# Odd heads' rows moved inside SBUF instead of repacked through DRAM, in a windowed-attention and MLP kernel

## The chip, the cores and the metric

The kernel runs on one core of one Trainium2 chip. The metric is the device time of one execution in microseconds (us).

Engines: PE multiplies matrices (PEld is its weight load), ACT applies activation functions, DVE is the vector engine, POOL is GpSimd, and SP (SyncE) issues the DMAs here. Each follows its own list of instructions, and between them they wait on semaphores.

## The reference

Two layers, each run twice with the same weights: attention over the last 256 positions with 32 heads of 16 numbers, and an MLP with GELU.

```python
def _A_ref(x, wqkv, wo):                      # x: 1 x 2048 x 512
    H = 32; Dh = 16; W = 256
    q, k, v = split(x @ wqkv)
    scores = einsum(q, k) * Dh ** -0.5        # masked to 0 <= i - j < W
    o = softmax(scores) @ v
    return o.reshape(B, S, D) @ wo
def _B_ref(x, w1, b1, w2, b2):                # F = 1792
    return gelu(x @ w1 + b1) @ w2 + b2

x = x + _A_ref(_layernorm(x), ...)
x = x + _B_ref(_layernorm(x), ...)            # both lines run twice
```

## The kernel before

Two parts matter. The first is the end of attention for one group of 8 heads and 256 queries; there are 64 groups. PV (the exponentials times the values) writes each head to a block of 17 PSUM rows at partition 32r, r = 0 to 3: 16 outputs, and in row 16 the sum of the exponentials (the value matrix has a column of ones). Even heads lie in the left half of the free axis (a = 0), odd heads in the right (a = 1). The output projection wants 128 dense rows, 8 heads times 16. So the group is copied to SBUF (OD) and repacked, while the sums take their own way.

```python
evac(lambda B: OD[:, s, :, :], ..., ["OD%d" % s], kind="o")        # s = group % 3; ACT or DVE
dma(Dc[:, rs, :] <- OD[16:P:32, s]  ("r a (k n) -> r (a k) n"))     # the sums, 8 KB; assumed 2.2 us
dma(scr[rs].rearrange("j r n -> r j n") <- OD[:, s])                # 256 KB to DRAM; assumed 3.8 us
add("dve", reciprocal(Rc[:, rs, :], Dc[:, rs, :]), prio=pr - 800)
dma(scr_r[rs] <- Rc[:, rs, :])                                      # 8 KB to DRAM; assumed 2.0 us
dma(On[:, rs, :] <- scr[rs, 0:Dh]   ("j r (a q) -> (j r a) q"))     # 128 KB, dense; assumed 2.3 us
dma(Rn[:, rs, :] <- scr_r[rs][None, :, :].to_broadcast([Dh, HC, 2*P]))  # 128 KB; assumed 2.8 us
add("pool", OT[:, bs, c, :] = On[:, rs, :] * Rn[:, rs, :], alt=dve) # POOL or DVE, input of the projection
```

(Written down shortly: `dma(a <- b)` stands for a helper with the same two access patterns. Dc holds the sums and Rc their reciprocals, Rn the reciprocals spread over 128 rows, On the repacked outputs, scr and scr_r are scratch in DRAM, scr_o in the profile; OT is the normalised output. "Dc landed" means that the DMA into Dc is complete.)

The second part is how the order of instructions comes about. The program is a graph of nodes with an assumed duration each. While the kernel is built, an ordering pass plays the graph through with these durations, and always starts the most urgent node that is ready:

```python
class _Plan:
    LAT = {"pe": 230.0, "act": 110.0, "dve": 110.0, "pool": 150.0, "sp": 100.0}
    def add(self, eng, fn, dur, reads=(), writes=(), prio=0.0, ...): ...
    def run(self):
        ...                                    # pick by priority among ready nodes
        nd["start"] = t
        end = t + dur
        efree[e] = t + nd["geo"] if e == "sp" else end     # geo: time to issue a DMA
        order.append(pick)
        ...
```

The result is one fixed list per engine. At run time nothing is picked again: if an instruction's input is late, all behind it on its engine wait (the timeline of POOL below shows a case).

The softmax here doesn't subtract the row's maximum and nothing guards it: scores larger than these inputs give would overflow.

## Time and profile before

| | before |
|---|---|
| time, median of 3 runs | 682.63 us (680.83 to 683.09) |
| profiled execution | 678.0 us |
| mean granted PE clock | 0.899 |

From the profile's page of the kernel before: busy time with its share of the span and the number of instructions, then the chain of waits, by engine and by line.

```profile
PE 516.0 (76%) x4945; PEld 250.9 (37%) x5008; DVE 368.4 (54%) x766; ACT 471.5 (70%) x701; POOL 269.2 (40%) x456
...
DMA 41%; PE 27%; ACT 15%; DVE 7%; SPq 5%; issue 3%; POOL 2%; DVEq 0%; POOLq 0%
DMA scr_o<-OD 22%; PE ps L544 21%; ACT E L647 13%; DMA Rn<-scr_r 12%; DMA scr_r<-Rc 5%; PE ps L690 3%; PE ps L634 2%; SPq L706 2%; PE ps L528 2%; SPq L715 1%; DMA X<-in_A_x_dram 1%; ACT OD L500 1%; DVE X L553 1%; DVE OT L723 1%; SPq L718 1%
```

No engine is full, and the chain is mostly DMA, half of it the store of the repack. Where PE idles stands in the groups of instructions; after the second bar is the idle time just before the group and what ended most of it. L634 is the scores, L690 is PV, L544 with Wo_sb the output projection, L528 the transposes of the normalised rows.

```profile
L634 PE MATMUL ps<-QT,KT 32*128 32x384 bf16 (+2 forms) x1024 | 92.1, 346 | 42.8 <-ACT E L647 41.6
...
L690 PE MATMUL ps<-E,Va 128*17 128x128 bf16 (+1 forms) x1920 | 60.5, 273 | 37.1 <-POOL E L660 16.6 <-DVE KT L588 7.0 <-DVE E L652 5.7
...
L544 PE MATMUL ps<-Wo_sb,OT 128*128 128x512 bf16 x120 | 36.7, 442 | 33.2 <-DVE OT L723 12.2 <-POOL OT L720 8.9 <-DVE Rc L711 6.4
...
L528 PE MATMUL ps<-ident,xn 128*128 128x128 bf16 x256 | 28.1, 245 | 23.5 <-DVE xn L520 20.9 <-DVE QT L498 1.5 <-DVE Va L498 0.8
```

Some matmul records are missing here (120 of 128 for Wo), so the idle times are a little too long.

Who waited for whom (total us, times, longest), kernel before; first the engines, then the DMA queue's own waits:

```profile
DVE OT L723 <- DMA Rn<-scr_r: 99.0, 30, 7.3
POOL OT L720 <- DMA Rn<-scr_r: 91.6, 29, 15.4
ACT E L647 <- PE ps L634: 85.5, 42, 23.7
```

```profile
SPq L715 <- DMA scr_o<-OD: 186.7, 61, 5.3
```

DVE and POOL stand still 191 us in total in front of OT, with 59 waits. SyncE spends 187 us waiting for the store before it may issue On. One group in the timeline of the DMA issues of the kernel before (start, duration of the issue, what):

```profile
285.90 0.58 SPq L706 DMA_DIRECT2D Dc<-OD  x1
286.52 0.55 SPq L709 DMA_DIRECT2D scr_o<-OD  x1
288.60 0.49 SPq L713 DMA_DIRECT2D scr_r<-Rc  x1
292.39 0.32 SPq L715 DMA_DIRECT2D On<-scr_o  x1
292.76 0.58 SPq L718 DMA_DIRECT2D Rn<-scr_r  x1
```

SyncE has nothing to do between 289.1 and 292.4: it waits until the store of 286.52 has landed, 5.87 us later. What one blocked OT does is best seen in the timeline of POOL, kernel before (the bracket: idle time before, and what ended it):

```profile
324.87 1.23 POOL L660 TENSOR_SCALAR_AFFINE_SELECT E<-E 128x512 bf16<-128x512 bf16 x2
334.69 0.72 POOL L720 TENSOR_TENSOR OT<-On,Rn 128x256 bf16<-128x256 f32 x1 [8.59 <-DMA Rn<-scr_r]
335.37 0.64 POOL L660 TENSOR_SCALAR_AFFINE_SELECT E<-E 128x512 bf16<-128x512 bf16 x1
```

The mask at 335.37 stood behind OT. PV needed the mask, and PE idled 8.5 us before it.

### The profile page before, as it was taken

Reading aid. Unit: us, or ns where it says so; the run is one execution under the profiler, and the core shown is the slowest. Engines: PE = TensorE matmul, PEld = TensorE weight load, DVE = VectorE, ACT = ScalarE, POOL = GpSimd, SP = SyncE. Lnnn points to the kernel's source line nnn. Section 1 sums busy time; section 2 is a strip of 40 time slices with the busy share of each in tenths; the row PEclk is TensorE's granted clock in tenths of the full one; section 3 lists DMA queues with packets and bytes.
Section 4 is the critical chain, followed back from the end, with each engine's and each line's share of the span. In section 5 each row is a group of like instructions: output and inputs, shape, how many; then the busy total and the mean of one; then the engine's idle time right before and its main releaser. Section 6 shows DMA issues by size and latency. Waiting matters only on the chain.

```text
span 678.0 us, 12448 instructions
## 1 busy us (share of the span) xinstructions
PE 516.0 (76%) x4945; PEld 250.9 (37%) x5008; DVE 368.4 (54%) x766; ACT 471.5 (70%) x701; POOL 269.2 (40%) x456
## 2 busy tenths in 40 slices
PE   3854778779467996799487988689768996589857
PEld 2421344344233433444133433434324433233524
DVE  6963646537474566735384666645565455624221
ACT  0497486859857897668486797669868795758503
POOL 5584333626533266312472265523544154401010
PEclk9975698989879998799798998799989998689979
DMA  9512221212322023212222022211322023211310
GB/s 291 176 49 74 71 65 28 56 49 55 77 64 64 18 65 81 66 31 67 64 67 63 18 72 68 57 47 45 93 73 66 21 79 83 70 55 43 85 41 23
DMA packets 47132, 45.38 MB, mean 67 GB/s; under 512 B 14049, under 2 KB 38370, under 8 KB 47074
## 3 DMA queue, kind: packets, MB, share of 16 engines
q1 hardware_dynamic: 47074, 44.59, 24.5%
q8 instruction: 39, 0.64, 0.4%
q14 instruction: 19, 0.16, 0.1%
HBM read 24.65 MB, written 19.40 MB: 65 GB/s over the span
## 4 chain that ended last, share of the span: by engine, by line
DMA 41%; PE 27%; ACT 15%; DVE 7%; SPq 5%; issue 3%; POOL 2%; DVEq 0%; POOLq 0%
DMA scr_o<-OD 22%; PE ps L544 21%; ACT E L647 13%; DMA Rn<-scr_r 12%; DMA scr_r<-Rc 5%; PE ps L690 3%; PE ps L634 2%; SPq L706 2%; PE ps L528 2%; SPq L715 1%; DMA X<-in_A_x_dram 1%; ACT OD L500 1%; DVE X L553 1%; DVE OT L723 1%; SPq L718 1%
## 5 line engine op out<-in xcount | busy, mean ns | idle before, releaser
L647 ACT ACTIVATE E<-ps 128x768 bf16<-128x768 f32 (+2 forms) x512 | 353.3, 786 | 87.3 <-PE ps L634 85.5
L660 POOL TENSOR_SCALAR_AFFINE_SELECT E<-E 128x512 bf16<-128x512 bf16 x221 | 162.2, 739 | 155.9 <-ACT E L647 155.5
L775 ACT ACTIVATE gT<-ps,b1T 128x512 bf16<-128x512 f32 (+1 forms) x140 | 81.3, 604 | 80.0 <-PE ps L544 79.5
L652 DVE TENSOR_TENSOR E<-E,mask 128x512 bf16<-128x512 bf16 x210 | 99.4, 476 | 48.5 <-ACT E L647 46.8
L634 PE MATMUL ps<-QT,KT 32*128 32x384 bf16 (+2 forms) x1024 | 92.1, 346 | 42.8 <-ACT E L647 41.6
L544 PE MATMUL ps<-W_sb,gT 128*128 128x512 bf16 x412 | 113.3, 388 | 4.2 <-issue 4.0
L544 PE MATMUL ps<-xnTB,W_sb 128*128 128x512 bf16 (+1 forms) x557 | 107.8, 343 | 2.3 <-DVE Va L498 1.1
L690 PE MATMUL ps<-E,Va 128*17 128x128 bf16 (+1 forms) x1920 | 60.5, 273 | 37.1 <-POOL E L660 16.6
L544 PE MATMUL ps<-xnTA,Wqkv_sb 128*128 128x256 bf16 x512 | 77.7, 299 | 7.3 <-DVE xnTA L498 3.1
L544 PEld LDWEIGHTS ps<-xnTB,W_sb 128*128 128x128 bf16 x560 | 54.1, 99 | 47.0 <-issue 5.1
L634 PEld LDWEIGHTS ps<-QT,KT 32*128 32x128 bf16 x1024 | 26.0, 92 | 121.0 <-ACT E L647 108.7
L553 DVE TENSOR_TENSOR X<-X,ps 128x512 bf16<-128x512 bf16 x64 | 43.7, 682 | 49.8 <-PE ps L544 49.5
L723 DVE TENSOR_TENSOR OT<-On,Rn 128x256 bf16<-128x256 f32 x33 | 16.1, 487 | 99.0 <-DMA Rn<-scr_r 99.0
L690 PEld LDWEIGHTS ps<-E,Va 128*17 128x17 bf16 x1920 | 42.3, 98 | 60.6 <-issue 21.0
L544 PE MATMUL ps<-Wo_sb,OT 128*128 128x512 bf16 x120 | 36.7, 442 | 33.2 <-DVE OT L723 12.2
L720 POOL TENSOR_TENSOR OT<-On,Rn 128x256 bf16<-128x256 f32 x31 | 24.6, 792 | 91.6 <-DMA Rn<-scr_r 91.6
L514 POOL TENSOR_SCALAR veps<-statmv 128x1 f32<-128x1 f32 x64 | 15.0, 235 | 112.3 <-DVE statmv L512 112.2
L544 PEld LDWEIGHTS ps<-xnTA,Wqkv_sb 128*128 128x128 bf16 x512 | 49.0, 106 | 28.6 <-issue 6.0
L544 PEld LDWEIGHTS ps<-W_sb,gT 128*128 128x128 bf16 x448 | 37.3, 98 | 49.4 <-issue 21.1
L528 PE MATMUL ps<-ident,xn 128*128 128x128 bf16 x256 | 28.1, 245 | 23.5 <-DVE xn L520 20.9
L510 DVE BATCH_NORM_STATS2 stat<-X 128x6 f32<-128x512 bf16 x64 | 43.5, 683 | 2.5 <-DMA X<-in_A_x_dram 2.0
L588 DVE TENSOR_TENSOR KT<-ps,parmask 128x1024 bf16<-128x1024 f32 x32 | 38.1, 1209 | 6.8 <-PE ps L544 6.8
(36 smaller groups left out, 366.8 us busy)
## 6 DMA issues: line engine op xcount, KB each, us to landing
scr_o<-OD SPq DMA_DIRECT2D x64, 256.0 KB
On<-scr_o SPq DMA_DIRECT2D x64, 128.0 KB
Rn<-scr_r SPq DMA_DIRECT2D x64, 128.0 KB
W_sb<-in_B_w_dram SPq DMA_DIRECT2D x2, 1792.0 KB
out_dram<-X SPq DMA_DIRECT2D x16, 128.0 KB
Wqkv_sb<-in_A_wqkv_dram SPq DMA_DIRECT2D x3, 512.0 KB
X<-in_A_x_dram SPq DMA_DIRECT2D x1, 1024.0 KB
Dc<-OD SPq DMA_DIRECT2D x64, 8.0 KB
```

What stands on the lines that cost most here:

```text
L510: add("dve", lambda e, B: e.bn_stats(stat6[:, k, :], X[:, t, :]), 620, reads=["X%d" % t], writes=["st%d" % k], prio=prio)
L528: r = e.transpose(psb[:, B[g][0], c * P : (c + 1) * P], xn[:, s, c * P : (c + 1) * P], ident[:])
L544: r = e.matmul(ps[:, B[g][0], cols], lhsT, rhs, start=st, stop=sp)
L553: add("dve", lambda e, B: e.tensor_tensor(out=X[:, t, :], in0=X[:, t, :], in1=ps[:, B[g][0], :], op=ALU.add), d_psum(512), reads=["X%d" % ...
L588: add("dve", lambda e, B, g=g, i=i: e.tensor_tensor(out=KT[:, kb, :, 2 * i : 2 * i + 2, :].rearrange("p a c q -> p a (c q)"), in0=ps[:, B[ ...
L634: x = e.matmul(ps[:, bk[r], 0:N], KT[rows, kb, par, c, j * P : (j + 1) * P], QT[rows, c, q0 : q0 + N], start=True, stop=True)
L647: a = (add("act", lambda e, B, g=g, gi=gi: e.activation(E[:, es, 2 * gi : 2 * gi + 2, 0:N], ps[:, B[g][0] : B[g][0] + 2, 0:N], AF.Exp, sca ...
L652: add("dve", lambda e, B: e.tensor_tensor(out=E[:, es, :, 0:P], in0=E[:, es, :, 0:P], in1=mask01[:, None, 0, :].to_broadcast([P, RG, P]), ...
L660: add("pool", lambda e, B: e.affine_select(E[:, es, :, 2 * P : 3 * P], E[:, es, :, 2 * P : 3 * P], [[0, RG], [-1, P]], ALU.is_ge, 0.0, bas ...
L690: x = e.matmul(ps[32 * r : 32 * r + VW, B[g][0], par * 256 + q_lo * P : par * 256 + (q_hi + 1) * P], Va[:, (2 * b + k) % VR, h, :], E[:, e ...
L720: add("pool", lambda e, B: e.tensor_tensor(out=OT[:, bs, c, :], in0=On[:, rs, :], in1=Rn[:, rs, :], op=ALU.mult), 750, reads=["On%d" % rs, ...
L775: gelu_last[0] = add("act", lambda e, B, g=g, fc=fc: e.activation(gT[:, fc, 0:M], ps[:, B[g][0], 0:M], AF.Gelu_apprx_tanh, bias=b1T[:, fc ...
```

## The change

Intent: leave out the trip through DRAM. Even heads already lie at partitions 32r to 32r+15. If the odd heads' 16 rows are moved up 16 partitions, to 32r+16 to 32r+31 of the left half, the rows are dense in the natural order. Row 16 of the left half holds the even heads' sum, so a move must wait until Dc has been read. OD now lives until OT is made, hence 5 buffers instead of 3. Rn is read in the new order, Wo with one plain load. The DMAs of the sums and reciprocals became more urgent for the ordering (`prio=pr - 50`), and the moves come after them. The assumed durations of the new nodes were chosen anew, so the static order differs on every engine.

```diff
-        OD = sb("OD", [P, 3, 2, 2 * P], dt.float32)
-        On = sb("On", [P, DC, 2 * P], dt.float32)
+        OD = sb("OD", [P, NOD, 2, 2 * P], dt.float32)                 # NOD = 5
...
-                dma(lambda e, B: e.dma_start(scr[rs].rearrange("j r n -> r j n"), OD[:, s].rearrange("p a q -> p (a q)")),
-                    ["S%d" % rs], reads=["OD%d" % s], prio=pr, dur=3800.0)
...
                 dma(lambda e, B: e.dma_start(scr_r[rs].rearrange("h (k n) -> (h k) n", n=32), Rc[:, rs, :]),
-                    ["SR%d" % rs], reads=["Rc%d" % rs], prio=pr, dur=2000.0)
-                dma(lambda e, B: e.dma_start(
-                    On[:, rs, :], scr[rs, 0:Dh].rearrange("j r (a q) -> (j r a) q", a=2)),
-                    ["On%d" % rs], reads=["S%d" % rs], prio=pr + 2, dur=2300.0)
-                dma(lambda e, B: e.dma_start(Rn[:, rs, :], scr_r[rs][None, :, :].to_broadcast([Dh, HC, 2 * P])),
-                    ["Rn%d" % rs], reads=["SR%d" % rs], prio=pr, dur=2800.0)
+                    ["SR%d" % rs], reads=["Rc%d" % rs], prio=pr - 50, dur=2000.0, issue=490.0)
+                dma(lambda e, B: e.dma_start(Rn[:, rs, :], scr_r[rs][:, None, :].to_broadcast([HC, Dh, 2 * P])),
+                    ["Rn%d" % rs], reads=["SR%d" % rs], prio=pr - 50, dur=3200.0, issue=580.0)
+                for r in range(RG):
+                    dma(lambda e, B, r=r: e.dma_start(
+                        OD[32 * r + Dh : 32 * r + 2 * Dh, s, 0, :], OD[32 * r : 32 * r + Dh, s, 1, :]),
+                        [ods[r]], reads=["Dc%d" % rs], prio=pr, dur=2200.0, issue=350.0)
                 add("pool", lambda e, B: e.tensor_tensor(
-                    out=OT[:, bs, c, :], in0=On[:, rs, :], in1=Rn[:, rs, :], op=ALU.mult), 750,
+                    out=OT[:, bs, c, :], in0=OD[:, s, 0, :], in1=Rn[:, rs, :], op=ALU.mult), 750,
```

## The prediction

> **What bounds the kernel now.** No engine is full: the page shows PE busy 516.0 of 678.0 us, ACT 471.5, DVE 368.4, POOL 269.2. PE sits idle about 162 us. The chain of waits is 41% DMA, and half of that (22% of the span) is the store scr_o<-OD of the DRAM repack. In the trace, that store takes 5.87 us from issue to landing (median), every time.
>
> Per group (64 of them), medians in the trace, counted from the end of the OD eviction: Dc lands at 3.0 us, the reciprocal starts at 3.6, scr_r<-Rc is issued at 3.9 and lands at 7.7, scr_o lands at 7.5, On and Rn are issued at 7.6 and 7.9, Rn lands and OT starts at 10.7 to 10.8. Two things stand out. scr_r, 8 KB, lands about 0.17 us after scr_o in most groups: alone it takes 1.7 us, behind scr_o 3.95 (median). And SyncE waits 186.7 us in all for scr_o before it may issue On (the DMA queue's own waits), which holds up the next group's Dc as well (up to 5.2 us).
>
> The Trainium skill, "DMA: Bandwidth & Descriptors", section "Why a DMA increments its semaphore by 16 and not by 1", says that the outermost sizes of both sides set how many DMA engines one transfer uses. scr_o's destination leads with 4 row groups, so 4 engines; the trace agrees (5 completion updates for it, 16 for On and Rn).
>
> The static order expected OT roughly 3 us earlier than it comes (its own costs give scr_o 3.8 us and Rn under 8 us after the eviction). So OT stands too early in two in-order queues: by the waits view DVE waits 99.0 us and POOL 91.6 us for Rn, in about 30 stalls each, while masks and evictions queue behind. PE pays: 27 us before the Wo matmuls (last one 6.8 us, at 650.8), 8.5 us at 336 (PV behind a POOL blocked by OT), and parts of the other PV and transpose stalls.
>
> **What changes.** Removed: the scr_o store and the On load. Added: four 16 KB moves per group on SyncE, about 0.35 us of issue each (On's issue is 0.32), landing in about 2 us (Dc: 1.94), beside the reciprocal's chain. Issue time per group rises from 2.5 to about 3.05 us; harmless. Rn now leads with 8 heads, so 8 engines: I estimate 3.0 us instead of 2.65. The single Wo load is worth nothing.
>
> New chain, estimated from those durations: Dc 2.0-2.3, reciprocal and issue 1.0, up to 0.7 behind moves, scr_r 1.75, Rn 3.0-3.2: OT at about 8.3 us instead of 10.8, and close to what the static order expects. Five OD buffers cover the longer life of OD.
>
> **Worth.** OT waits on DVE and POOL should fall from 190 to 60-90 us. Of the 35 us of PE stalls named and some 20 us of related ones I expect 25-35 us back; the tail alone about 5 us. ACT's exponentials (353 us) and PE keep the rest.
>
> Predicted: 652 us, 8-in-10 range 632 to 671. Faster by over 2%: 0.82; within 2%: 0.15; slower: 0.03.
>
> **Signs.** Right: OT about 8 to 9 us after the eviction; scr_r landing in 1.7-2.2 us; Rn near 3 us; DVE and POOL waits for Rn more than halved; PE idle below 140 us; chain with DMA share well under 41%. Wrong: scr_r still near 4 us; moves landing after Rn; SyncE waiting on moves or Dc for long.
>
> **What would make it wrong.** The moves holding scr_r or the next Dc back on SyncE; a worse static order by chance (1 to 2%); waits for OT that were covered by exponentials anyway, so that shortening them buys little; a lower granted clock with denser matmuls.

## The result, and the profile after

The kernel after takes 617.16 us (median of 4 runs, 615.2 to 618.95); before, in the same rounds, 681.73 us. The ratio is 0.905, with a 95% interval of 0.901 to 0.909. Ratios here are the mean time of one kernel's fast runs over that of the other's of the same rounds, so they are not quite the ratio of the medians quoted. Executions over 1.5% slower than the fastest of the same kernel are left out of the means. The result is correct, and faster than the predicted range of 632 to 671 us.

The page of the kernel after, the same lines as before:

```profile
PE 513.6 (84%) x5008; PEld 246.0 (40%) x5008; DVE 369.5 (60%) x770; ACT 472.4 (77%) x704; POOL 272.7 (44%) x449
...
PE 43%; ACT 24%; DMA 15%; SPq 8%; DVE 6%; issue 2%; POOL 1%; DVEq 0%; POOLq 0%
PE ps L541 33%; ACT E L644 20%; SPq L714 6%; DMA Dc<-OD 6%; DMA Rn<-scr_r 5%; PE ps L631 4%; PE ps L687 4%; DMA scr_r<-Rc 3%; DMA X<-in_A_x_dram 2%; ACT L644 1%; PE ps L525 1%; ACT OD L497 1%; ACT gT L772 1%; DVE KT L585 1%; DVE X L550 1%
```

The engines do the same work. What went is idle time: PE's fell from 162.0 us (678.0 - 516.0) to 100.7 us (614.3 - 513.6). The same PE groups, kernel after (line numbers are 3 less):

```profile
L631 PE MATMUL ps<-QT,KT 32*128 32x384 bf16 (+2 forms) x1024 | 92.4, 347 | 47.9 <-ACT E L644 46.6
...
L687 PE MATMUL ps<-E,Va 128*17 128x128 bf16 (+1 forms) x1920 | 60.1, 273 | 11.1 <-DVE KT L585 2.6 <-DVE E L649 2.5 <-POOL E L653 1.6
L541 PE MATMUL ps<-Wo_sb,OT 128*128 128x512 bf16 x128 | 35.8, 414 | 11.1 <-DVE OT L720 5.3 <-POOL OT L717 4.2 <-DVE KT L585 0.9
...
L525 PE MATMUL ps<-ident,xn 128*128 128x128 bf16 x256 | 26.0, 231 | 13.5 <-DVE xn L517 12.3 <-DVE Va L495 0.8 <-DVE xnTA L495 0.3
```

PV lost as much idle time as the projection that reads OT: 26.0 us against 22.1. PV does not read OT; it waits for masks and evictions, which are made by engines that stood in front of OT (as in the POOL timeline above). The wait for exponentials (L631) did not shrink. Waits in the kernel after, engines and then the DMA queue:

```profile
DVE OT L720 <- DMA Rn<-scr_r: 54.9, 22, 6.5
...
POOL OT L717 <- DMA Rn<-scr_r: 26.9, 21, 4.1
```

```profile
SPq L714 <- DMA Dc<-OD: 66.4, 50, 2.4
```

The waits of OT for any DMA fell from 190.6 to 86.8 us (81.8 of them for Rn). SyncE now waits for Dc before the first move. One group in its timeline, kernel after:

```profile
111.82 0.61 SPq L704 DMA_DIRECT2D Dc<-OD  x1
113.63 1.19 SPq L714 DMA_DIRECT2D OD<-OD  x2
114.92 0.53 SPq L709 DMA_DIRECT2D scr_r<-Rc  x1
115.49 1.23 SPq L714 DMA_DIRECT2D OD<-OD  x2
116.81 0.65 SPq L711 DMA_DIRECT2D Rn<-scr_r  x1
```

A move takes 0.59 us to issue (median of 256), not 0.35, and in every group at least two moves stand before the reciprocals' store (two in 23 groups, three in 24, all four in 17).

The medians of the 64 groups, in us after the end of the eviction unless the row says otherwise (from the traces of the two kernels; the predicted issue is the sum of the prediction's terms):

| | before | after | predicted |
|---|---|---|---|
| Dc landed | 3.0 | 2.1 | 2.0-2.3 |
| reciprocals' store issued | 3.9 | 4.4 | 3.0-4.0 |
| it landed, from its issue | 3.95 | 1.74 | 1.75 |
| Rn landed, from its issue | 2.65 | 2.74 | 3.0-3.2 |
| OT starts | 10.80 | 9.74 | 8.3 |

That is the puzzle: OT came only 1.06 us earlier, less than half of what was predicted, and the gain was twice the predicted one.

### The profile page after: what moved, and what is told of

Its sections match the earlier page's. It is cut to its first block, busy times and chain, and to the rows that moved or that the text cites. A ratio compares the mean times of both kernels' runs of the same rounds, so it can differ in the third digit from the quotient of the medians.

```text
span 614.3 us, 12794 instructions
## 1 busy us (share of the span) xinstructions
PE 513.6 (84%) x5008; PEld 246.0 (40%) x5008; DVE 369.5 (60%) x770; ACT 472.4 (77%) x704; POOL 272.7 (44%) x449
## 4 chain that ended last, share of the span: by engine, by line
PE 43%; ACT 24%; DMA 15%; SPq 8%; DVE 6%; issue 2%; POOL 1%; DVEq 0%; POOLq 0%
PE ps L541 33%; ACT E L644 20%; SPq L714 6%; DMA Dc<-OD 6%; DMA Rn<-scr_r 5%; PE ps L631 4%; PE ps L687 4%; DMA scr_r<-Rc 3%; DMA X<-in_A_x_dram 2%; ACT L644 1%; PE ps L525 1%; ACT OD L497 1%; ACT gT L772 1%; DVE KT L585 1%; DVE X L550 1%
## 5 line engine op out<-in xcount | busy, mean ns | idle before, releaser
L657 POOL TENSOR_SCALAR_AFFINE_SELECT E<-E 128x512 bf16<-128x512 bf16 x216 | 165.2, 767 | 138.8 <-ACT E L644 137.6
L649 DVE TENSOR_TENSOR E<-E,mask 128x512 bf16<-128x512 bf16 x210 | 100.4, 479 | 58.2 <-ACT E L644 56.0
L631 PE MATMUL ps<-QT,KT 32*128 32x384 bf16 (+2 forms) x1024 | 92.4, 347 | 47.9 <-ACT E L644 46.6
L541 PE MATMUL ps<-W_sb,gT 128*128 128x512 bf16 x448 | 121.0, 382 | 0.0
L541 PE MATMUL ps<-xnTB,W_sb 128*128 128x512 bf16 (+1 forms) x560 | 109.6, 341 | 0.7 <-ACT gT L772 0.5
L541 PE MATMUL ps<-xnTA,Wqkv_sb 128*128 128x256 bf16 x512 | 75.0, 293 | 6.9 <-DVE xnTA L495 3.9
L631 PEld LDWEIGHTS ps<-QT,KT 32*128 32x128 bf16 x1024 | 26.1, 92 | 125.3 <-ACT E L644 112.3
L687 PE MATMUL ps<-E,Va 128*17 128x128 bf16 (+1 forms) x1920 | 60.1, 273 | 11.1 <-DVE KT L585 2.6
L720 DVE TENSOR_TENSOR OT<-OD,Rn 128x256 bf16<-128x256 f32 x35 | 18.0, 515 | 56.6 <-DMA Rn<-scr_r 54.9
L541 PE MATMUL ps<-Wo_sb,OT 128*128 128x512 bf16 x128 | 35.8, 414 | 11.1 <-DVE OT L720 5.3
L653 POOL TENSOR_SCALAR_AFFINE_SELECT E<-E 128x512 bf16<-128x512 bf16 x46 | 30.9, 671 | 24.2 <-ACT E L644 24.1
L497 ACT ACTIVATE OD<-ps 128x512 f32<-128x512 f32 x34 | 20.7, 610 | 26.3 <-PE ps L687 26.2
L514 POOL TENSOR_TENSOR rstd<-veps,mhalf 128x1 f32<-128x1 f32 x64 | 37.5, 587 | 4.1
```

Of the source, the lines that this page charges most:

```text
L514: add("pool", lambda e, B: e.tensor_tensor(out=rstd[:, k : k + 1], in0=veps[:, k : k + 1], in1=mhalf[:], op=ALU.pow), 590, reads=["ve%d" % ...
L541: r = e.matmul(ps[:, B[g][0], cols], lhsT, rhs, start=st, stop=sp)
L631: x = e.matmul(ps[:, bk[r], 0:N], KT[rows, kb, par, c, j * P : (j + 1) * P], QT[rows, c, q0 : q0 + N], start=True, stop=True)
L649: add("dve", lambda e, B: e.tensor_tensor(out=E[:, es, :, 0:P], in0=E[:, es, :, 0:P], in1=mask01[:, None, 0, :].to_broadcast([P, RG, P]), ...
L653: alt=(("pool", lambda e, B: e.affine_select(E[:, es, :, 0:P], E[:, es, :, 0:P], [[0, RG], [1, P]], ALU.is_ge, 0.0, base=0, channel_multip ...
L657: add("pool", lambda e, B: e.affine_select(E[:, es, :, 2 * P : 3 * P], E[:, es, :, 2 * P : 3 * P], [[0, RG], [-1, P]], ALU.is_ge, 0.0, bas ...
```

## The experiments

Theory A: what costs time is not how long OT takes but how much later it comes than the static order expects, since then it blocks DVE and POOL for everything behind it. Theory B: the slow transfers cost time in any order, by latency, traffic and the blocked DMA queue. Theory B': it is the slow store alone, not DRAM as such. Theory C: evictions waited for an output buffer.

To judge A, the expected start of OT is needed. The ordering pass computes it: the median over the 64 groups, and the length that it gives the whole program. These two are assumptions of the kernel, not measurements, and are marked "expected".

| kernel | OT expected | OT measured | late by | whole, expected | time, median | ratio to before |
|---|---|---|---|---|---|---|
| before | 8.19 | 10.80 | 2.61 | 593 | 681.7 | 1 |
| b_jitter | 8.18 | 10.86 | 2.68 | 590 | 682.2 | 1.001 |
| b_od5 | 8.19 | 10.64 (slow) | | 593 | 679.6 (3 fast runs) | 0.996 |
| b_true_costs | 10.02 | 12.63 | 2.61 | 596 | 659.0 | 0.967 |
| b_late_plan | 12.93 | 13.57 | 0.64 | 602 | 627.3 | 0.920 |
| b_store8 | 8.19 | 8.72 | 0.53 | 593 | 610.3 | 0.896 |
| b_store16 | 8.19 | 8.07 | -0.12 | 593 | 591.8 | 0.868 |
| b_store16_ok | 8.17 | 8.31 | 0.14 | 593 | 596.6 | 0.876 |
| s16_true | 7.43 | 8.45 | 1.02 | 590 | 607.1 | 0.891 |
| s16_late | 8.49 | 8.54 | 0.05 | 593 | 593.3 | 0.869 |
| after | 8.79 | 9.74 | 0.95 | 598 | 617.2 | 0.905 |
| a_od3 | 8.79 | 9.46 | 0.67 | 598 | 617.8 | 0.908 |
| a_true_costs | 8.06 | 8.58 | 0.52 | 589 | 608.2 | 0.893 |
| a_rn2 | 8.79 | 12.52 | 3.73 | 598 | 704.4 | 1.032 |

Before, b_store8, b_store16 and b_od5 have the same order of instructions on PE, ACT, DVE, POOL and SyncE, checked line by line; so have after, a_od3 and a_rn2.

The waits of OT for DMAs, summed over DVE and POOL in each profile, tell how much the two engines were blocked: 190.5 us before, 185.3 in b_jitter, 153.6 in b_true_costs, 105.3 in b_store8, 100.4 in s16_true, 93.1 in a_true_costs, 90.2 in b_late_plan, 86.8 after, 84.5 in a_od3, 76.5 in b_store16_ok, 67.2 in b_store16, 56.1 in s16_late and 189.5 in a_rn2. They follow the times roughly, not strictly: of the runs between 84 and 106 us the one with 90.2 is the slowest.

### b_true_costs: the ordering's costs corrected

```diff
-  Dc dur=2200.0              scr dur=3800.0              SR dur=2000.0              On dur=2300.0              Rn dur=2800.0
+  Dc dur=1940.0, issue=580   scr dur=5870.0, issue=550   SR dur=3950.0, issue=490   On dur=2000.0, issue=320   Rn dur=2650.0, issue=580
```

> The kernel before, with the same transfers; only the costs that the static ordering assumes for its five transfers are set to the trace's medians (Dc 1.94, store 5.87, reciprocal store 3.95, On 2.00, Rn 2.65 us). Theory A (the loss was a static order that expects OT too early, so that OT blocks DVE and POOL): most of the gain comes back, 645 us or less, with OT still about 10.5 us after the eviction and the waits for Rn on DVE and POOL under 100 us together. Theory B (the loss was the DRAM transfers' latency, traffic and the blocked DMA queue themselves): 665 us or more.

Measured: 659.04 us, ratio 0.967 (0.962 to 0.972). This lies between the two theories. Of theory A's side conditions, one failed: OT came at 12.63 us, not 10.5. The waits for Rn were under 100 us as it asked (79.6), but OT now waited 74.0 us for On too, 154 us together. In the new order some transfers took longer (the reciprocals' store 4.35 us, On 2.34), and OT was again 2.6 us later than expected. Knowing the old durations was not enough: they changed with the order.

### b_store16: the same order, the store on 16 DMA engines

The Trainium skill, "DMA: Bandwidth & Descriptors", section "Why a DMA increments its semaphore by 16 and not by 1", says that a transfer uses the largest number of DMA engines up to 16 that divides the slowest dimension of both sides. The store's destination led with r, 4. With r outside of j in the scratch, r and j merge to 128:

```diff
-        scr = nc.dram_tensor("scr_o", (4, 32, RG, 4 * P), dt.float32, kind="Internal").ap()
+        scr = nc.dram_tensor("scr_o", (4, RG, 32, 4 * P), dt.float32, kind="Internal").ap()
-            scr[rs].rearrange("j r n -> r j n") <- OD
+            scr[rs].rearrange("r j n -> (r j) n") <- OD
-            On <- scr[rs, 0:Dh].rearrange("j r (a q) -> (j r a) q", a=2)
+            On <- scr[rs, :, 0:Dh].rearrange("r j (a q) -> (j a) r q", a=2)      # heads permuted: wrong result
```

> The kernel before in the same static order on every engine; the repack still goes through DRAM with the same bytes, but the scratch layout lets the store spread over 16 DMA engines (heads come out permuted, so the result is wrong on purpose). Store expected at 2.3 to 2.8 us instead of 5.87, the reciprocals' store at 1.7 to 2.2 instead of 3.95. Theory B' (it is the slow 4-engine store and what it holds up, not DRAM as such): OT about 8.5 us after the eviction and 620 to 640 us. If the gain needs the moves inside SBUF or the new order: 660 us or more.

Measured: 591.82 us, ratio 0.868 (0.863 to 0.874). Its output is wrong, which doesn't matter for the time. One layout of a scratch buffer, with the same bytes through DRAM and the same order, gave more than the whole change, and more than expected (620 to 640 us, OT about 8.5 us; it came at 8.07). On's load changed its pattern too, against the gain: 0.60 us to issue and 2.44 to land, before 0.32 and 2.00. The store landed in 2.15 us instead of 5.87 and the reciprocals' store in 1.69 instead of 3.95. The chain of waits of b_store16:

```profile
PE 47%; ACT 35%; DVE 7%; DMA 6%; POOL 2%; issue 2%; SPq 1%; DVEq 0%; POOLq 0%
PE ps L544 37%; ACT E L647 30%; PE ps L634 5%; PE ps L690 3%; DMA Rn<-scr_r 2%; DVE X L553 2%; DMA X<-in_A_x_dram 2%; ACT L647 2%; ACT OD L500 1%; PE ps L528 1%; DMA scr_o<-OD 1%; DVE KT L588 1%; ACT gT L775 1%; DVE stat L510 1%; DMA scr_r<-Rc 1%
```

The store fell from 22% of the chain to 1%. One group of its DMA issues:

```profile
271.56 0.58 SPq L706 DMA_DIRECT2D Dc<-OD  x1
272.19 0.45 SPq L709 DMA_DIRECT2D scr_o<-OD  x1
275.03 0.48 SPq L713 DMA_DIRECT2D scr_r<-Rc  x1
275.56 0.60 SPq L715 DMA_DIRECT2D On<-scr_o  x1
276.72 0.54 SPq L718 DMA_DIRECT2D Rn<-scr_r  x1
```

On no longer waits for the store, and Rn is out 5.2 us after Dc, not 6.9.

### b_od5 and a_od3: the number of output buffers alone

```diff
-        OD = sb("OD", [P, 3, 2, 2 * P], dt.float32)      # b_od5; s = od_rr[0] % 3
+        OD = sb("OD", [P, 5, 2, 2 * P], dt.float32)      #        s = od_rr[0] % 5
-    NOD = 5                                              # a_od3
+    NOD = 3
```

> The kernel before in the same static order, with 5 output buffers instead of 3 and nothing else. Theory C (evictions waited for an output buffer): 660 us or less. Theories A and B: within 1% of the kernel before, 676 to 683 us.

> The kernel after in the same static order, with 3 output buffers instead of 5. In it a buffer lives until OT is made, about 10 us, with one eviction every 6 to 10 us. Theory C: 640 us or more. Theories A and B: 617 to 630 us.

Measured: b_od5 676.8, 679.6 and 680.7 us in its fast runs (a fourth, the profiled one, was slow: 696.6 us at a clock of 0.787), ratio 0.996 (0.990 to 1.003). a_od3 617.83 us, ratio 0.908 (0.902 to 0.914), like the kernel after. Theory C falls on both sides: the five buffers did nothing.

### b_late_plan: the slow transfers untouched, the order told to expect OT late

```diff
   (as b_true_costs, but)
-  Rn dur=2650.0
+  Rn dur=5650.0
```

> The kernel before with its slow DRAM repack untouched; only the static ordering's assumed costs are changed, now 3 us too long for Rn (5.65 us), so that it expects OT 12.9 us after the eviction, about when it came in b_true_costs (12.6). Theory A (what costs time is OT coming later than the static order expects): 600 to 635 us although OT is as late as ever. Theory B (the slow transfers cost time in any order, through buffers and the blocked queue): 650 us or more.

Measured: 627.29 us, ratio 0.920 (0.917 to 0.923), correct. OT came at 13.57 us, 2.8 us later than in the kernel before, and the store took 6.03 us, and still 54 us were gained. This separates A from one half of B: with every transfer as slow as before or slower in the median, most of the gain is there once the order expects it. It does not hold the DMA queue fixed: in the new order SyncE waited 39.9 us for the store, not 186.7 (and 71.5 us for the reciprocals' store). So latency and traffic are not the main cost, unless this order was a lucky one (see b_jitter); the blocked queue is not ruled out. The waits of OT fell to 90.2 us, by this order, in which the median Rn lands 2.0 us before OT starts:

```profile
DVE OT L723 <- DMA On<-scr_o: 34.2, 13, 6.0
POOL OT L720 <- DMA On<-scr_o: 29.8, 9, 18.9
DVE OT L723 <- DMA Rn<-scr_r: 18.8, 6, 5.1
POOL OT L720 <- DMA Rn<-scr_r: 7.5, 4, 5.2
```

The DMA queue's own wait in this run:

```profile
SPq L715 <- DMA scr_o<-OD: 39.9, 18, 3.7
```

The page of b_late_plan and its groups for PV and the projection:

```profile
PE 521.4 (83%) x5008; PEld 247.8 (39%) x5008; DVE 377.4 (60%) x774; ACT 469.6 (75%) x701; POOL 268.6 (43%) x448
```

```profile
L690 PE MATMUL ps<-E,Va 128*17 128x128 bf16 (+1 forms) x1920 | 59.7, 269 | 14.2 <-POOL E L656 5.5 <-POOL E L660 5.2 <-DVE statmv L512 1.2
...
L544 PE MATMUL ps<-Wo_sb,OT 128*128 128x512 bf16 x128 | 35.9, 415 | 7.5 <-DVE OT L723 3.8 <-DVE Va L498 2.6 <-POOL OT L720 1.0
```

The projection's idle time is now less than in the kernel after, although OT is 3.8 us later than there.

### b_store8: a dose in between

```diff
-        scr = nc.dram_tensor("scr_o", (4, 32, RG, 4 * P), ...)
+        scr = nc.dram_tensor("scr_o", (4, 8, 17, 4 * P), ...)
-            scr[rs].rearrange("j r n -> r j n") <- OD
+            scr[rs, :, 0:16, :] <- OD
-            On <- scr[rs, 0:Dh].rearrange("j r (a q) -> (j r a) q", a=2)
+            On <- scr[rs, 0:8:2, 0:Dh].rearrange("r j (a q) -> (j a) r q", a=2)  # wrong result again
```

> As b_store16, same static order, but the scratch layout leads with 8, so 8 DMA engines carry the store (result again permuted, wrong on purpose). Store expected near 3.4 us (between 2.15 on 16 and 5.87 on 4). If the number of DMA engines is what counts: OT 8.2 to 9.2 us after the eviction and 595 to 625 us. If it was something else in the new layout (HBM addresses): 670 us or more.

Measured: 610.31 us, ratio 0.896 (0.892 to 0.899). The store took 4.05 us, not 3.4; OT came at 8.72 us. The completion updates of the store in the traces are 5, 9 and 16 for the three layouts (4 and 8 DMA engines plus one update by the issuer, and 16), which agrees with the skill. In one fixed order the time thus follows the store: 5.87, 4.05, 2.15 us give 681, 610, 592 us. It isn't linear: the first 1.8 us bring 71 us, the next 1.9 us bring 18, since there OT is only 0.5 us late.

### b_jitter: the luck of the order

```diff
-    LAT = {"pe": 230.0, "act": 110.0, ...}
+    LAT = {"pe": 230.0, "act": 150.0, ...}
```

> A control for the luck of the static order: the kernel before, with the ordering's assumed latency after an ACT instruction at 150 ns instead of 110. That changes hundreds of places in the order of PE, DVE and POOL, but not when OT is expected (8.2 us after the eviction, as before). Theory A: 667 to 695 us, because OT still comes 2.6 us later than expected. If the differences seen so far are luck of the order: could fall anywhere, also under 650 us.

Measured: 682.21 us, ratio 1.001 (0.996 to 1.007). Hundreds of places in the order changed, the lateness did not, nor did the time. One control doesn't measure the spread of all orders, and b_true_costs, in another order and just as late, is 3.3% faster. So a difference of a few per cent between two orders may be chance; those within one order (b_store8 and b_store16 against before, a_rn2 against after, 10 to 14%) can't be. For b_late_plan, 8% in an order of its own, chance is unlikely and not excluded.

### a_rn2: the kernel after, made late

```diff
-   Rn[:, rs, :] <- scr_r[rs][:, None, :].to_broadcast([HC, Dh, 2 * P])
+   Rn[:, rs, :] <- scr_r[rs, 0:2][:, None, :].to_broadcast([2, P // 2, 2 * P])    # wrong result
```

> The kernel after in the same static order, with Rn read as 2 rows by 64 partitions, so that only 2 DMA engines carry it (the result is wrong on purpose). Rn expected to land 2.5 to 5 us later than its 2.74 us, so OT some 3 us or more later than in the kernel after. Theory A: the gain goes again, 660 us or more, with large waits for Rn on DVE and POOL, though not a byte goes through the DRAM repack. If the gain of the change was in the removed traffic and not in when OT comes: 640 us or less.

Measured: 704.40 us, ratio 1.032 (1.028 to 1.037). Same order as the kernel after, no repack through DRAM, and it is slower than the kernel before. Rn landed in 4.53 us, 1.8 more than in the kernel after (2.5 to 5 were expected), but OT came 2.8 us later: Dc now took 3.42 us instead of 1.81. The skill's section named above says that a DMA with k engines takes the lowest-numbered k, and "Queues, rings and completion order" that each DMA engine consumes its descriptors in ring order; so Dc (4 engines) would queue behind an earlier group's Rn on 2. The records here count the engines (3 completion updates for Rn) but don't name them, so this is an explanation, not a finding; the 3.42 us is measured. The waits of OT in a_rn2:

```profile
DVE OT L720 <- DMA Rn<-scr_r: 105.4, 29, 7.6
...
POOL OT L717 <- DMA Rn<-scr_r: 73.4, 26, 6.9
```

### a_true_costs: the rest of the loss in the kernel after

```diff
-  Dc dur=2200.0, issue=580   SR dur=2000.0, issue=490   Rn dur=3200.0, issue=580   moves dur=2200.0, issue=350
+  Dc dur=1830.0, issue=610   SR dur=1740.0, issue=540   Rn dur=2740.0, issue=640   moves dur=1810.0, issue=600
```

> The kernel after, same transfers, with the static ordering's costs set to its own trace's medians (Dc 1.83, reciprocal store 1.74, Rn 2.74, moves 1.81 us with 0.60 us of issue instead of 0.35). Theory A: the rest of the loss against the order's own expectation goes, 595 to 610 us, with the reciprocals' store issued before the third move. If the moves themselves or their issue time are the limit: 613 us or more.

Measured: 608.24 us, ratio 0.893 (0.890 to 0.895), correct: 9 us better than the kernel after, by four pairs of numbers. The reciprocals' store left before the third move in 55 of 64 groups (in the kernel after in 23; in 17 it left after the fourth), and OT came at 8.58 us, near the 8.3 us that the prediction had named. But the mechanism that was expected did not show: the loss against the order's own length was to go, and it is as large as before (608 - 589 = 19 us; in the kernel after 617 - 598 = 19), though OT is only 0.52 us late; the waits of OT even rose from 86.8 to 93.1 us. The time fell by as much as the order's own length did. Four costs were changed together, so the share of the moves' issue time isn't shown, and 1.5% between two orders may be chance.

### b_store16_ok, s16_true, s16_late: a correct kernel with the spread store

On with one DMA can't keep the head order (its source would need four dimensions), so two DMAs load it, one for each parity:

```diff
-                dma(On[:, rs, :] <- scr[rs, 0:Dh].rearrange("j r (a q) -> (j r a) q", a=2))
+                for a in range(2):
+                    dma(On[a:P:2, rs, :] <- scr[rs, :, 0:Dh, a*2*P : (a+1)*2*P].rearrange("r j q -> j r q"))
   (s16_true, also)
+  Dc 1800/590   scr 2130/450   SR 1700/490   On 2260/590   Rn 2570/540        (dur/issue, ns)
   (s16_late: as s16_true, but)
+  Rn 3870/540
```

> b_store16 with a correct result: On is loaded by two DMAs, one for each head parity, into every second partition, which keeps the head order. One more issue per group on SyncE (0.3 to 0.6 us). Theory B' : within 2% of b_store16, 590 to 604 us, and faster than the kernel after. If SyncE's issue time is what held the kernel after back: nearer 610 us.

> b_store16_ok (store on 16 DMA engines, On in two loads, correct) with the ordering's costs set to its own trace's medians. It then expects OT 7.4 us after the eviction, less than the 8.2 of b_store16_ok and less than the 8.3 measured there. Theory A: no better than b_store16_ok, 594 to 615 us, if OT still comes 0.5 to 1 us later than expected; better (588 us or less) only if OT comes as early as expected.

> As s16_true with Rn assumed 1.3 us longer than measured, so that OT is expected 8.5 us after the eviction. Theory A: OT comes within 0.3 us of the expected time or earlier, and the time is 585 to 600 us, no worse than s16_true.

Measured, all correct: b_store16_ok 596.61 us, ratio 0.876 (0.874 to 0.879); s16_true 607.11 us, 0.891 (0.885 to 0.898); s16_late 593.34 us, 0.869 (0.865 to 0.874). With the costs at the exact medians it came out slower than b_store16_ok (the intervals of the two ratios lie apart), and 1.3 us of slack on Rn made it 14 us faster. Medians leave out the waits between issues: s16_true expects to issue Rn 4.53 us after the eviction and OT at 7.43 us; it issues Rn at 5.65 and gets OT at 8.45, although its DMAs land as fast as assumed (Rn in 2.52 us). s16_late expects 8.49 and gets 8.54. It is the best correct kernel of this study, 12.9% under the kernel before by medians (593.34 against 681.10 us); b_store16_ok is close, and came from another call, so I don't rank the two. The page of s16_late:

```profile
PE 509.5 (86%) x5008; PEld 244.2 (41%) x5008; DVE 367.9 (62%) x763; ACT 472.7 (80%) x707; POOL 278.8 (47%) x453
...
PE 48%; ACT 31%; DVE 9%; DMA 6%; SPq 2%; issue 2%; POOL 2%; POOLq 0%; DVEq 0%
```

DMA is down to 6% of the chain; PE and ACT make up 79% of it.

### What stays open

- How the loss of the kernel before divides between the late store itself, the reciprocals' store stuck behind it, and SyncE waiting for it. No run changed one of them alone; b_late_plan comes nearest (store and reciprocals' store as slow as before, SyncE's wait for the store down to 39.9 us).
- b_true_costs is as late as the kernel before (2.61 us) and 22 us faster. Its waits of OT are less (154 us against 191), so the lateness of a median isn't the whole story; why this order turns the same lateness into fewer waits is open.
- Why 0.5 us of lateness still goes with a loss of 17 to 19 us in b_store8 and a_true_costs, no less than 1.0 us in the kernel after and s16_true.
- Why a move takes 0.59 us to issue and On took 0.32.

## Why the prediction was wrong

Right, in direction and cause: the change was faster, the store and what hung on it was the cause, and the static order "expected OT roughly 3 us earlier than it comes" (2.61 us). These signs came true:

- The reciprocals' store landed in 1.74 us (1.7 to 2.2 predicted), Rn in 2.74 us ("near 3 us").
- OT's waits on DVE and POOL fell from 190.6 to 86.8 us (60 to 90 predicted).
- PE idled 100.7 us (below 140 predicted); DMA has 15% of the chain, not 41%.
- The tail: PE's idle time before the last group's Wo fell from 6.83 to 1.54 us ("about 5 us" predicted).

Wrong:

- **The step that failed is the size of the last one: "Of the 35 us of PE stalls named and some 20 us of related ones I expect 25-35 us back."** The three groups of matmuls behind DVE and POOL gave back 58.1 us: the projection 22.1 (33.2 to 11.1), PV 26.0 (37.1 to 11.1), the transposes 10.0 (23.5 to 13.5). The scores took 5.1 us more. The span fell by 63.7 us. The stalls directly before Wo were counted nearly right (27 us, of which 22.1 came back). On PV and the transposes the prediction counted 8.5 and some 20 us, and 36.0 came back there, of 60.6 us of idle time: what a blocked DVE or POOL hands on was taken to be small, and was the larger part. And the gain was counted as if about half of the stalls would stay, but as much came back as it had counted in all (55 us): OT's lateness fell by 64%, from 2.61 to 0.95 us, and the loss against the order's expectation fell with it, from 89 us (682 - 593) to 19 us (617 - 598).
- "OT at about 8.3 us" was wrong in the other direction: 9.74 us. The moves take 0.59 us of SyncE each, not "about 0.35", which was taken from On's 0.32; the reciprocals' store left at 4.4 us, behind two to four of them. With the costs corrected (a_true_costs), OT came at 8.58 us and the time was 9 us less.
- One sign against the prediction did come: "SyncE waiting on moves or Dc for long". SyncE waited 66.4 us for Dc before the first move. It did not undo the gain: before, SyncE had waited 186.7 us for the store.
- "Waits for OT that were covered by exponentials anyway" was named as the risk. It did not come: PE's idle time before the scores, nearly all of it for exponentials, rose by only 5.1 us while 58.1 us elsewhere went.
- "A lower granted clock with denser matmuls" did not come either: the mean granted clock in the profiled runs went up, 0.899 to 0.925, and to 0.939 in s16_late.
- The intent of the change, to avoid DRAM, was not the cause of the gain. The repack through DRAM with the store on 16 DMA engines is faster than the moves (b_store16_ok 596.6, after 617.2, a_true_costs 608.2 us). The five buffers gave nothing (b_od5, a_od3).

The Trainium skill, "DMA: Bandwidth & Descriptors", section "Rules for kernel authors", has both points that I didn't weigh: that an outermost dimension under 16 confines a DMA to at most as many engines (the prediction names the 4 engines of the store, but did not ask what the store would take on 16), and that transfers under 64 KB are mostly overhead. This agrees with the second too: one 16 KB move lands in 1.81 us, the spread 256 KB store in 2.15 us, and four moves take 2.4 us of issue.

## What to carry to other kernels

In a kernel whose order is fixed beforehand, compare when each late input arrives with when the order expected it: measured against the order's own expected length, here 0.05 us late cost nothing measurable, 0.5 to 1.0 us 17 to 25 us, 2.6 us 63 to 92 us and 3.7 us 106 us in 64 groups, with slow transfers and fast ones. Either make the transfer as fast as assumed or assume it as slow as it is, waits between the issues included, and rather a microsecond too much (that last rests on one pair of runs, s16_true and s16_late). Before a DMA is designed away, look at how many DMA engines it uses: the leading dimension of a scratch layout was worth more than the whole detour.

## What the Trainium skill lacked or had wrong

- "DMA: Bandwidth & Descriptors", the rules on the number of engines: right (3, 5, 9 and 16 completion updates for 2, 4, 8 and 16 engines), but without landing times by the number of engines. Here a 256 KB store from SBUF to DRAM landed in 5.87, 4.05 and 2.15 us on 4, 8 and 16 engines (the 8-engine layout also had padded rows).
- The same page doesn't say what a narrow transfer does to others: an 8 KB store took 1.69 us beside the spread store and 3.95 us beside the 4-engine one; Dc took 1.81 us, and 3.42 us when Rn ran on 2 engines (medians).
- No page gives a time, measured on this chip, for which SyncE is held by one DMA, or says that it depends on the access pattern. The same page has the sequencer's dispatch on the other path ("Anatomy of one DMA — SWDGE (gpsimd) path", about 50 ns) and, in its part on trn3, a cycle count for earlier generations in passing. Here SyncE was held 0.32 to 0.64 us per DMA (medians: On 0.32 before and 0.60 in b_store16's pattern, reciprocals' store 0.49, Dc 0.58, moves 0.59, Rn 0.58 before and 0.64 after).
- No page compares a move between partitions of SBUF with a trip through DRAM: 16 rows of 1 KB landed in 1.81 us; a spread store and a load took 2.15 and 2.44 us.
